# Two quarters of M made in one stay of TensorE, and keys asked for three steps ahead of their transposes

## The chip, the core and the metric

The kernel runs on one core of a Trainium2 chip. The metric is the time of one execution in microseconds, taken on the device, as the median of the runs shown. The profile is one further execution, recorded by the hardware profiler; its times are microseconds from the start of its span. The engines are called by the profile's names: PE (matmuls) and PEld (its weight loads), DVE, ACT and POOL (elementwise work), SP (here the issuer of the DMAs; its queue is SPq).

## What is computed

Eight batches of attention with 8 heads of 64, 576 tokens each, in two stages, and a feed-forward layer behind it. `p` holds 32 queries for each head.

```python
import numpy as np

def sm_attn(qq, kk, vv):
    s = scale * np.matmul(qq, kk.transpose(0, 1, 3, 2))
    s = s - np.max(s, axis=-1, keepdims=True)
    a = np.exp(s)
    a = a / (np.sum(a, axis=-1, keepdims=True) + 1e-09)
    return np.matmul(a, vv)

p_packed = sm_attn(p, k, v)                # 32 rows for each head
out = sm_attn(q, p_packed, p_packed)       # 576 rows for each head
x = out.transpose(0, 2, 1, 3).reshape(B * S, H * D)      # 4608 x 512
h = x @ w_in                               # 512 x 2048
relu6 = np.clip(h + 3.0, 0.0, 6.0)
y = (h * relu6 / 6.0) @ w_out              # 2048 x 512
```

All inputs and the output are float32.

## The kernel before

**Algebra.** Since `out` is a weighted sum of 32 packed rows for each head, `x @ w_in` is computed as attention weights times **M**, where M is the packed rows times `w_in` (256 x 2048 for each batch, as 8 heads of 32 rows). M is made in four **quarters** of 512 columns, n = 0 to 3. `u_m` (L528) makes a quarter: PE multiplies the packed rows (`pps`) with a quarter of `w_in` in `each_head` (L336, the matmul is L350), in its shape of 64x32 rows and columns, in 16 small matmuls, which the profile shows as 16 records. Such a visit of PE to this shape is called a **stay** here. Then two copies for each of two PSUM banks follow: ACT writes `m_hi` (L537), DVE the remainder `m_lo` (L539). The same `each_head` also makes scores of keys and queries with 288 columns in a stay.

**A batch.** The batches are worked one after the other; the work of batch b + 1's attention and M is laid in between the steps of batch b. A batch has two chunks of tokens, c = 0 and 1, and each chunk 16 steps, one for every 128 columns of d_ff; s = 16c + f counts the 32 steps. In even batches chunk 0 has 256 tokens (narrow) and chunk 1 has 320 (wide); in odd ones it is the other way round. A step begins with `fill` (L1401), which calls what is laid in there. Then PE makes the first product (`first_product` L922, matmul L929: attention weights as `a_hi`, `a_lo` times `m_hi`, `m_lo`, six matmuls) in one of two PSUM tiles, ACT and DVE make the gate h * relu6(h + 3) out of it (L940, L941), and the second product with `w_out` follows two or more steps later (L969). Twelve of the steps form six **pairs** (`moe_pairs` L1106), whose second products go through combined weights, as in a Strassen step: `wt` tiles T1, T2 and T4 of a pair. Of these `wt1` and `wt2` change hands: `FETCHES` (L29 to L33) and `fetch_t` (L1103, L1104) bring 768 KB from DRAM (`t_kept`) into `wt2` at step 5 and into `wt1` at step 7 of chunk 0, and back in chunk 1. Gates of a pair are t (first step) and tb (second step); ge, gf and ga are their parts that PE takes. Chunk 0 takes the pairs from the last to the first, so pairs 5 and 4 come first.

**M of the next batch.** A quarter of `w_in` is fetched anew for each batch from a copy in DRAM, 1 MB (`fetch_w_in` L1378, L1380, tile `w_again`, for which there is one place). `first_quarters` (L1382) fetches quarters 2, 1 and 0, each followed by its stay and its copies; `fill` takes one part of it at every step from 21 on (the stays come at steps 23, 28 and 31), and at step 31 all that is left of it, and then fetches quarter 3. Quarter 3's stay and its copies come as `late` at steps 1 to 3 of the next batch.

**Keys and queries.** `attention_inputs` (L558) loads the keys of the batch after, four times 4 DMAs of 72 KB (L294, tile `nat`, two places), and DVE transposes each into a tile `tr` (L555, four places): the loads of keys 0 and 1 stand at step 0, the four transposes at steps 1 to 4, the load of keys 2 and 3 behind the transposes of keys 0 and 1. Queries follow in the same tiles.

**What sets the order.** The program is written in steps, but the order of the instructions on each engine, SP's queue among them, is settled by a scheduler when the kernel is built, except where the matmuls of a stay or second products are placed by hand. Each engine then works its queue in order and waits at the head of it.

## Time and profile before

| what | before |
|---|---|
| runs, us | 712.67, 714.36, 715.0 |
| median, us | 714.36 |
| profiled execution, us | 714.05 |
| its span, us | 712.3 |
| PE busy, us and instructions | 690.8, 5906 |
| DVE busy | 533.8, 1164 |
| ACT busy | 429.5, 1015 |
| POOL busy | 349.7, 542 |

The span is the stretch between the first and the last instruction that the profiler saw; the execution's own time is a little longer. Busy time is the sum of an engine's durations without overlap. The page's row of slices (40 of 17.8 us) shows PE at 60% and 50% in the first two and at 90% or more in all behind them but the last, at 70%; its clock row stands at 9 tenths or more from the third on. In a row of a timeline the first two numbers are start and duration, then come engine, line, operation, output<-input tiles, form and count; a bracket at the end holds how long the engine had been idle ahead of it, and who ended that. A line "DMA to landing" gives the time from the issue of DMAs to the arrival of their data. A wait row reads: engine, tile and line, who was waited for, us in total, how often, the longest.

### The profile page before, as it was taken

How to read it: one execution, taken by the hardware profiler on the slowest of the kernel's cores; microseconds unless marked ns; L12 is line 12 of the kernel's file. 1: busy time of each engine (PE TensorE's matmuls, PEld its weight loads, DVE VectorE, ACT ScalarE, POOL GpSimd, SP SyncE). 2: the span in 40 equal slices, each digit the busy share in tenths (PEclk: the TensorE clock that was granted, in tenths of full speed). 3: DMA queues.
4: the chain of work that ended last, by engine and by line, in shares of the span. 5: the costliest groups of instructions: out<-in, count | busy, mean ns of one | idle time of the engine just before them, and what ended most of it. 6: DMA issues, size and time to landing. Idle time of an engine off the chain costs nothing.

```text
span 712.3 us, 16083 instructions
## 1 busy us (share of the span) xinstructions
PE 690.8 (97%) x5906; PEld 593.8 (83%) x5906; DVE 533.8 (75%) x1164; ACT 429.5 (60%) x1015; POOL 349.7 (49%) x542
## 2 busy tenths in 40 slices
PE   6599999999999999999999999999999999999997
PEld 4377877887878988899898988889898898889997
DVE  2887788688999769886598867887488776975453
ACT  5798876455565656566465655657366564756453
POOL 1565542545353454465353544556354444547553
PEclk9699999999999999999999999999999999999999
DMA  9989853955237756474454657375543845331030
GB/s 281 301 222 230 230 128 117 262 146 133 96 119 184 172 140 213 112 171 94 115 203 128 160 119 215 119 155 130 127 164 119 169 119 178 119 134 46 31 104 29
DMA packets 199102, 107.48 MB, mean 151 GB/s; under 512 B 173424, under 2 KB 185200, under 8 KB 195440
## 3 DMA queue, kind: packets, MB, share of 16 engines
...
q10 hardware_dynamic: 544, 0.20, 0.1%
...
## 4 chain that ended last, share of the span: by engine, by line
PE 75%; DVE 7%; DMA 3%; ACT 2%; issue 1%; SPq 1%; POOL 1%; DVEq 0%; ACTq 0%
PE acc L969 42%; PE ps_hh L929 23%; PE ps L350 6%; PE ps L969 2%; DVE tr L555 1%; PE ps L470 1%; PE ps_h L607 1%; DMA raw_out<-in_moe_w_out_dram 1%; DVE wt L1076 1%; DMA nat<-in_q_dram 1%; DMA w_again<-w_kept 1%; DMA nat<-in_k_dram 1%; SPq L294 1%; PE ps L440 0%; ACT wt L1075 0%
## 5 line engine op out<-in xcount | busy, mean ns | idle before, releaser
L929 PE MATMUL ps_hh<-a_hi,m_hi 128*128 128x320 f32 (+1 forms) x448 | 134.0, 299 | 0.6 <-DVE tb L941 0.4
L929 PE MATMUL ps_hh<-a_lo,m_hi 128*128 128x320 f32 (+1 forms) x448 | 133.3, 298 | 0.0
L929 PE MATMUL ps_hh<-a_hi,m_lo 128*128 128x320 f32 (+1 forms) x448 | 132.8, 296 | 0.0
L941 DVE SCALAR_TENSOR_TENSOR t<-t,ps_hh 128x320 f32<-128x320 f32 (+1 forms) x148 | 65.9, 446 | 56.4 <-ACT t L940 55.8
L947 POOL TENSOR_TENSOR gf<-tb,gf 128x256 fp32r<-128x256 f32 x76 | 64.2, 845 | 88.0 <-ACT gf L946 51.9
L969 PE MATMUL acc<-wo_hi,g 128*128 128x512 f32 x288 | 103.3, 401 | 0.0
L940 ACT ACTIVATE t<-ps_hh,three 128x320 f32<-128x320 f32 (+1 forms) x148 | 73.8, 500 | 32.4 <-PE ps_hh L929 27.3
L929 PEld LDWEIGHTS ps_hh<-a_hi,m_hi 128*128 128x128 f32 x448 | 84.6, 189 | 8.4 <-DVE t L941 1.9
L929 PEld LDWEIGHTS ps_hh<-a_lo,m_hi 128*128 128x128 f32 x448 | 84.7, 189 | 6.5 <-issue 3.5
L929 PEld LDWEIGHTS ps_hh<-a_hi,m_lo 128*128 128x128 f32 x448 | 84.5, 189 | 2.9 <-issue 2.5
L947 POOL TENSOR_TENSOR g<-t,g 128x256 fp32r<-128x256 f32 x72 | 54.8, 763 | 45.4 <-ACT g L946 24.4
L969 PE MATMUL acc<-wt,ga 128*128 128x256 f32 x456 | 74.7, 284 | 0.5 <-ACT ga L946 0.4
L969 PE MATMUL acc<-wo_hi,ge 128*128 128x256 f32 x304 | 71.8, 287 | 1.0 <-ACT ge L946 0.8
L947 POOL TENSOR_TENSOR ga<-t,ga 128x256 fp32r<-128x256 f32 x76 | 62.3, 820 | 13.5 <-ACT ga L946 12.3
L969 PEld LDWEIGHTS acc<-wt,ga 128*128 128x128 f32 x456 | 63.0, 190 | 3.7 <-ACT ga L946 1.7
L969 PEld LDWEIGHTS acc<-wo_hi,g 128*128 128x128 f32 x288 | 53.1, 188 | 13.0 <-POOL g L947 3.4
L969 PEld LDWEIGHTS acc<-wo_hi,ge 128*128 128x128 f32 x304 | 52.9, 190 | 9.6 <-DVE t L941 2.5
L969 PE MATMUL acc<-wo_lo,g 128*128 128x512 f32 x144 | 57.0, 396 | 0.0
L965 POOL COPY bnd<-t 128x64 f32<-128x64 f32 x76 | 22.3, 294 | 69.3 <-DVE t L941 66.5
L555 DVE STREAM_TRANSPOSE tr<-nat 128x576 f32<-128x576 f32 x56 | 42.3, 763 | 16.9 <-DMA nat<-in_q_dram 11.7
L940 ACT ACTIVATE tb<-ps_hh,three 128x256 f32<-128x256 f32 (+1 forms) x76 | 37.9, 498 | 19.4 <-PE ps_hh L929 18.4
L947 POOL TENSOR_TENSOR edge<-bnd,edge 128x256 fp32r<-128x256 f32 (+1 forms) x50 | 32.8, 662 | 32.2 <-ACT edge L946 32.2
...
## 6 DMA issues: line engine op xcount, KB each, us to landing
w_again<-w_kept SPq DMA_DIRECT2D x24, 1024.0 KB, 4.9
...
w_kept<-w_in_sb SPq DMA_DIRECT2D x4, 1024.0 KB, 8.9
```

Source lines behind the costliest of these rows:

```text
L294: nc.sync.dma_start(out=t[r:r + 32], in_=src[b, 2 * a + h, :, 32 * c:32 * c + 32].rearrange("(t i) j -> i t j", i=32),)
L350: nc.tensor.matmul(pair[x][NPK * a:NPK * a + NPK, :n], rows[half, a], c, start=True, stop=True)
L470: nc.tensor.matmul(pair[x][cols, :D], l, r, start=(c == 0), stop=(c == NST - 1))
L555: nc.vector.transpose(out=t, in_=state.pop(("nat", which, b, a)))
L607: nc.tensor.matmul(h[:, hf, :HS], mm[:, g, fs], aa[:, hf * HS:(hf + 1) * HS], start=(g == 0 and i == 0), stop=(g == NG - 1 and i == 2),)
L929: state["first"] = nc.tensor.matmul(h[:, :n], mm[:, g, fs], aa[:, t0:t0 + n], start=(g == 0 and i == 0), stop=(g == NG - 1 and i == 2),)
L940: state["relu"] = nc.scalar.activation(out=t[:, :n], in_=h, func=AF.Relu, bias=three)
L941: state["gate"] = nc.vector.scalar_tensor_tensor(out=t[:, :n], in0=t[:, :n], scalar=6.0, in1=h, op0=ALU.min, op1=ALU.mult)
L947: engine.tensor_sub(out=lo, in0=x, in1=hi.bitcast(F32))
L965: nc.gpsimd.tensor_copy(out=bnd[:, f, side * REM:side * REM + REM], in_=t[:, boff:boff + REM])
L969: nc.tensor.matmul(out, lhs[x], rhs[y], start=first and i == 0, stop=last and i == 2, skip_group_check=True)
L1076: nc.vector.tensor_sub(out=lo, in0=made, in1=hi.bitcast(F32))
```

## The change

Quarter 2 of the next batch's M is fetched at step 22, its stay moves to step 24, its copies to steps 27 and 28. Quarters 1 and 0 are fetched at step 24, right behind that stay. Quarter 1 goes into the tiles of the transposed keys and queries, which become one tile of four parts (`all_turned`), quarter 0 into the place of `w_again`. At step 31 both are multiplied in one stay, quarter 1 in two spare banks. One copy pair of quarter 1 follows at the same step, the other at step 0 of the next batch, those of quarter 0 at steps 2 and 3; quarter 3 is fetched at step 4, and has its stay at step 6 and its copies at 7 and 8. For b > 2 the keys' transposes start two steps later, at step 3 instead of 1, while the loads of keys 0 and 1 stay at step 0. Batch 1's M is made as before.

```diff
--- before.py
+++ after.py
@@ -24,6 +24,7 @@
 LATE = (3, 2, 1, 2, 1)
+SOON = (22, 24, 27, 28, 31, 31)
 PAIRS = 6
@@ -285,6 +286,18 @@
+    shared = []
+
+    def all_turned():
+        return ap.tile([P, 4, S], F32, name="tr", tag="tr", bufs=1)
+
+    def turned_room():
+
+        if not shared:
+            t = all_turned()
+            shared.extend(t[:, i] for i in range(4))
+        return shared.pop(0)
...
@@ -551,7 +564,7 @@
     def turn(which, b, a):
-        t = ap.tile([P, T, 32], F32, name="tr", tag="tr", bufs=4)
+        t = turned_room().rearrange("p (t n) -> p t n", n=32)
         nc.vector.transpose(out=t, in_=state.pop(("nat", which, b, a)))
@@ -561,6 +574,9 @@
         load("k", b, 0)
         load("k", b, 1)
         yield
+        if b > 2:
+            yield
+            yield
         transpose_p(b)
...
@@ -878,7 +894,7 @@
         def in_tr():
-            return ap.tile([P, 4 * P], F32, name="rows0", tag="tr", bufs=4)
+            return turned_room()[:, :4 * P]
@@ -1375,28 +1391,39 @@
-    def fetch_w_in(n):
-        t = w_in_sb[n] = wr.tile([P, FPC, NPAIR, P], F32, name="w_again", tag="w_in0")
+    def fetch_w_in(n, turned=False):
+        if turned:
+            t = all_turned().rearrange("p i n -> p (i n)")[:, :FPC * DM]
+            t = t.rearrange("p (f a e) -> p f a e", f=FPC, a=NPAIR)
+        else:
+            t = wr.tile([P, FPC, NPAIR, P], F32, name="w_again", tag="w_in0")
+        w_in_sb[n] = t
         nc.sync.dma_start(out=t.rearrange("p f a e -> p (f a e)"), in_=w_kept[n])
 
-    def first_quarters(b):
-
-        for n in range(NCH - 2, -1, -1):
-            fetch_w_in(n)
-            yield
-            yield
-            yield from coarse(u_m(b, n))
-
+    def quarters(b):
+
+        fetch_w_in(2)
+        yield
+        parts = coarse(u_m(b, 2))
+        next(parts)
+        fetch_w_in(1, True)
+        fetch_w_in(0)
+        yield
+        yield from parts
+        yield from coarse(u_m(b, 0, 1))
+        fetch_w_in(NCH - 1)
+        yield
+        yield
+        yield from coarse(u_m(b, NCH - 1))
+
+    soon = coarse(part for n in range(1, NCH) for part in u_m(1, n))
     for b in range(1, B):
         more = b + 1 < B
+        late, soon = soon, quarters(b + 1) if more else iter(())
...
         if b == 1:
-            late = coarse(part for n in range(1, NCH) for part in u_m(1, n))
             turned = [combine(i) for i in range(PAIRS)]
-        else:
-            late = coarse(u_m(b, NCH - 1))
-        soon = first_quarters(b + 1) if more else iter(())
...
-                    if s > 0:
+                    if s != 1:
                         next(late, None)
...
-                if s >= 21:
+                for _ in range(SOON.count(s)):
                     next(soon, None)
-                if s == 31 and more:
-                    rest(soon)
-                    fetch_w_in(NCH - 1)
```

Three places show what the order becomes. Rows name line, operation, output<-input with the tiles' numbers, and the shape; the diff moves later lines down by 13 to 16, so L350 of before is L363, L929 is L945, L941 is L957, L969 is L985 and L555 is L568.

**PE at the end of batch 2.** Before, around the stay of quarter 0 for batch 3; `g2` are the gates of batch 2's last single steps, `ps_hh` the first products of batch 3:

```order
L969 MATMUL acc_3598<-wo_lo_723,g2_3951 128x512
L969 MATMUL acc_3602<-wo_hi_722,g2_3951 128x512
L969 MATMUL acc_3602<-wo_lo_723,g2_3951 128x512
L350 MATMUL ps2_4007<-w_again_4005,pps_83 32x512 x8
L969 MATMUL acc_3598<-wo_hi_722,g2_3951 128x512
L969 MATMUL acc_3602<-wo_hi_722,g2_3951 128x512
L929 MATMUL ps_hh_4062<-a_hi_3728,m_hi_3773 128x320
L929 MATMUL ps_hh_4062<-a_lo_3729,m_hi_3773 128x320
```

After, at the same place:

```order
L985 MATMUL acc_3579<-wo_lo_719,g2_3956 128x512
L363 MATMUL ps_x_3968<-tr_3750,pps_83 32x512
L363 MATMUL ps_x_3967<-tr_3750,pps_83 32x512
L363 MATMUL ps_x_3968<-tr_3750,pps_83 32x512
L363 MATMUL ps_x_3967<-tr_3750,pps_83 32x512
L363 MATMUL ps_x_3968<-tr_3750,pps_83 32x512
L363 MATMUL ps_x_3967<-tr_3750,pps_83 32x512
L363 MATMUL ps_x_3968<-tr_3750,pps_83 32x512
L363 MATMUL ps_x_3967<-tr_3750,pps_83 32x512
L363 MATMUL ps2_3966<-w_again_3752,pps_83 32x512 x8
L985 MATMUL acc_3575<-wo_hi_718,g2_3956 128x512
L985 MATMUL acc_3579<-wo_hi_718,g2_3956 128x512
L945 MATMUL ps_hh_4050<-a_hi_3693,m_hi_3836 128x320
```

The stay of quarter 1, which stood 62 rows earlier, now goes ahead of quarter 0's with no full matmul between them.

**DVE at the start of batch 2.** Before, from behind the first gate `t_2870` of the batch to the end of that pair's gates; `p_tr` is the transpose of `p`, `wt2` and `wx` belong to the making of the combined weights, `osb` to the output of batch 1:

```order
L1196 TENSOR_TENSOR t_2870<-t_2870 128x128
L322 STREAM_TRANSPOSE p_tr_2895<-p_nat_2848 128x128
L555 STREAM_TRANSPOSE tr_2897<-nat_2853 128x576
L1095 TENSOR_TENSOR wx_2743<-wx_2743,wo_lo_723 128x256
L941 SCALAR_TENSOR_TENSOR tb_2911<-tb_2911,ps_hh_2904 128x256
L1167 SCALAR_TENSOR_TENSOR osb_2645<-acc_2421,osb_2645 128x512
L947 TENSOR_TENSOR ge_2874<-t_2870,ge_2874 128x256
L1167 SCALAR_TENSOR_TENSOR osb_2646<-acc_2425,osb_2646 128x512
L1204 TENSOR_TENSOR t_2870<-t_2870,tb_2911 128x2x128
L1076 TENSOR_TENSOR wt2_1789<-wx_2743,wt2_1789 128x256
L941 SCALAR_TENSOR_TENSOR t_2952<-t_2952,ps_hh_2945 128x256
L1209 TENSOR_TENSOR tb_2911<-tb_2911,t_2870 128x128
```

After, from the same gate `t` on:

```order
L957 SCALAR_TENSOR_TENSOR t_2845<-t_2845,ps_hh_2838 128x256
L1111 TENSOR_TENSOR wx_2718<-wx_2718,wo_lo_719 128x256
L1212 TENSOR_TENSOR t_2845<-t_2845 128x128
L1092 TENSOR_TENSOR wt2_1777<-wx_2718,wt2_1777 128x256
L963 TENSOR_TENSOR ge_2849<-t_2845,ge_2849 128x256
L957 SCALAR_TENSOR_TENSOR tb_2865<-tb_2865,ps_hh_2858 128x256
L1183 SCALAR_TENSOR_TENSOR osb_2628<-acc_2406,osb_2628 128x512
L1220 TENSOR_TENSOR t_2845<-t_2845,tb_2865 128x2x128
L1183 SCALAR_TENSOR_TENSOR osb_2629<-acc_2410,osb_2629 128x512
L1225 TENSOR_TENSOR tb_2865<-tb_2865,t_2845 128x128
L552 TENSOR_TENSOR m_lo_2889<-ps2_2776,m_hi_2888 128x512
L957 SCALAR_TENSOR_TENSOR t_2899<-t_2899,ps_hh_2892 128x256
```

The transposes of `p` and of keys 0, which stood between the first gate and its `ge`, come behind these gates and those of the next pair (three and four rows further on; the second keys ten rows further on).

**DVE at the start of batch 4, after,** where keys 2 and 3 are transposed (`nat_5406` and `nat_5459`):

```order
L957 SCALAR_TENSOR_TENSOR tb_5492<-tb_5492,ps_hh_5485 128x256
L1220 TENSOR_TENSOR t_5471<-t_5471,tb_5492 128x2x128
L963 TENSOR_TENSOR ge_5475<-t_5471,ge_5475 128x256
L1225 TENSOR_TENSOR tb_5492<-tb_5492,t_5471 128x128
L568 STREAM_TRANSPOSE tr_5404<-nat_5406 128x576
L957 SCALAR_TENSOR_TENSOR t_5558<-t_5558,ps_hh_5551 128x256
L1212 TENSOR_TENSOR t_5558<-t_5558 128x128
L552 TENSOR_TENSOR m_lo_5566<-ps2_5526,m_hi_5565 128x512
L568 STREAM_TRANSPOSE tr_5404<-nat_5459 128x576
L963 TENSOR_TENSOR ge_5562<-t_5558,ge_5562 128x256
L957 SCALAR_TENSOR_TENSOR tb_5577<-tb_5577,ps_hh_5570 128x256
L1220 TENSOR_TENSOR t_5558<-t_5558,tb_5577 128x2x128
```

Before, these two stood two steps earlier; now they are ahead of the gates of the fourth pair that PE takes.

**SP at the start of batch 3.** Before, from the fetch of quarter 3 (`w_again_4025`) on; `nat` are keys and queries, `v_nat` values, `osb` the output:

```order
L1380 DMA w_again_4025<-w_kept_1573 128x2048
L294 DMA nat_4099<-in_k_dram 32x18x32 x4
L1170 DMA out_0_dram<-osb_3976 128x512
L1170 DMA out_0_dram<-osb_3977 128x512
L294 DMA nat_4141<-in_k_dram 32x18x32 x4
L294 DMA nat_4165<-in_q_dram 32x18x32 x4
L419 DMA v_nat_4223<-in_v_dram 128x4x64 x2
L294 DMA nat_4218<-in_q_dram 32x18x32 x4
L419 DMA v_nat_4223<-in_v_dram 128x4x64 x2
L409 DMA v_nat_4223<-in_v_dram 64x4x64 x2
L1104 DMA wt2_1789<-t_kept_1574 128x1536
```

After:

```order
L1401 DMA w_again_4157<-w_kept_1564 128x2048
L1186 DMA out_0_dram<-osb_3939 128x512
L1186 DMA out_0_dram<-osb_3940 128x512
L1120 DMA wt2_1777<-t_kept_1565 128x1536
L307 DMA nat_4106<-in_k_dram 32x18x32 x4
L307 DMA nat_4160<-in_k_dram 32x18x32 x4
L432 DMA v_nat_4247<-in_v_dram 128x4x64 x2
L307 DMA nat_4182<-in_q_dram 32x18x32 x4
L307 DMA nat_4242<-in_q_dram 32x18x32 x4
L432 DMA v_nat_4247<-in_v_dram 128x4x64 x2
L422 DMA v_nat_4247<-in_v_dram 64x4x64 x2
L1120 DMA wt1_1776<-t_kept_1565 128x1536
```

Keys 2 and 3 (`nat_4106`, `nat_4160`) now stand behind the fetch of `wt2`, which stood behind keys, queries and values before; the starts of batches 2, 4, 5 and 6 have the same order.

## The prediction

> **What bounds the kernel now.** I read the page's engine shares first, then the chain that ended last, then the windows of PE by batch, and only then single rows.
>
> ```profile
> span 712.3 us, 16083 instructions
> PE 690.8 (97%) x5906; PEld 593.8 (83%) x5906; DVE 533.8 (75%) x1164; ACT 429.5 (60%) x1015; POOL 349.7 (49%) x542
> PE 75%; DVE 7%; DMA 3%; ACT 2%; issue 1%; SPq 1%; POOL 1%; DVEq 0%; ACTq 0%
> 551.00:635.00 84.00, 83.72 (x752) 1.00 0.52 143
> L350 PE MATMUL ps<-w_again,pps 64*32 64x512 f32 x384 | 26.1, 601 | 0.0
> ```
>
> PE is busy for 690.8 of 712.3 us and carries 75% of the chain. The window row (PE's busy time as sum and mean with its instructions, its clock, the DMA share, GB/s) is one whole batch of 84 us: PE has gaps of 0.3 us in it, at full clock. So a microsecond counts only if PE issues less, or if PE stops waiting. Batch time hides small waits, because a modelled duration overlaps the next start; I therefore count from start to start. The last row is the work that the change regroups: the stays of PE in its 64x32 shape that make M, 24 of 16 records each.
>
> **Part 1, the merged stay.** What a stay costs is read between the last full matmul ahead of it and the second one behind it.
>
> ```profile
> 385.70 0.28 PE L929 MATMUL ps_hh<-a_lo,m_hi 128*128 128x256 f32 x1
> 385.82 0.28 PE L929 MATMUL ps_hh<-a_hi,m_lo 128*128 128x256 f32 x1
> 386.02 1.09 PE L350 MATMUL ps<-w_again,pps 64*32 64x512 f32 x16
> ...
> 387.27 0.28 PE L969 MATMUL acc<-wo_lo,ge 128*128 128x256 f32 x1
> ...
> 399.99 0.28 PE L929 MATMUL ps_hh<-a_hi,m_lo 128*128 128x256 f32 x1
> 400.20 0.72 PE L350 MATMUL ps<-tr,p_tr 64*32 64x288 f32 x16
> ...
> 401.07 0.28 PE L969 MATMUL acc<-wo_lo,gf 128*128 128x256 f32 x1
> ```
>
> ```profile
> 56.01 0.39 PE L969 MATMUL acc<-wo_hi,gl 128*128 128x512 f32 x1
> 56.33 0.71 PE L350 MATMUL ps_w<-tr,p_tr 64*32 64x288 f32 x16
> ...
> 57.80 0.40 PE L969 MATMUL acc<-wo_lo,gh 128*128 128x512 f32 x1
> 58.03 0.39 PE L969 MATMUL acc<-wo_hi,gl 128*128 128x512 f32 x1
> ```
>
> A 256-column matmul follows the next at 0.12 us (385.70 to 385.82), a 512-column one at 0.23 (57.80 to 58.03). One M stay is thus (387.27 − 0.12) − (385.82 + 0.12) = 1.21 us. One stay of 288 columns is (401.07 − 0.12) − (399.99 + 0.12) = 0.84. The trace of before has no two M rounds in one stay, but it has two rounds of 288 columns in one (the second, left out, is 16 records too): (57.80 − 0.23) − (56.01 + 0.23) = 1.33 us, against 2 x 0.84 = 1.68. The second round saves 0.35 us, the price of entering and leaving the shape once. That does not depend on the columns, so two M rounds in one should take 2 x 1.21 − 0.35 = 2.07. The change merges quarters 0 and 1 for b = 2 to 7: 6 x 0.35 = **−2.1 us**, bounds 0 (all comes back, rival 3) and −2.1.
>
> The work the merged stay issues is otherwise the same: the same 32 records, the same four copies. The fetches stay the same three megabytes; from quarter 2's stay at step 24 to the merged one at step 31 there are seven steps of 84/32 = 2.6 us, and a fetch lands in 4.9:
>
> ```profile
> w_again<-w_kept SPq DMA_DIRECT2D x24, 1024.0 KB, 4.9
> ```
>
> Two behind one another are some 10 us against 18: hidden. Quarter 3's fetch waits for the merged stay and has from step 31 to step 6, seven steps again. I cost the fetches at nothing.
>
> **Part 2, waits that the new times remove.** At the start of b = 2, PE waits for gates that stand on DVE behind three key transposes (the first and the last of them below) and copies of quarter 0.
>
> ```profile
> 216.87 0.28 PE L929 MATMUL ps_hh<-a_hi,m_lo 128*128 128x256 f32 x1
> 217.75 0.39 PE L969 MATMUL acc<-wo_hi,ge 128*128 128x256 f32 x1 [0.60 <-ACT ge L946]
> ...
> 223.03 0.32 PE L969 MATMUL acc<-wo_hi,ga 128*128 128x256 f32 x1
> 223.56 0.39 PE L969 MATMUL acc<-wo_hi,ge 128*128 128x256 f32 x1 [0.20 <-ACT ge L946]
> ...
> 224.00 0.28 PE L969 MATMUL acc<-wo_lo,ge 128*128 128x256 f32 x1
> 224.71 0.39 PE L929 MATMUL ps_hh<-a_hi,m_hi 128*128 128x256 f32 x1 [0.43 <-DVE tb L941]
> ```
>
> ```profile
> 217.40 0.74 DVE L555 STREAM_TRANSPOSE tr<-nat 128x576 f32<-128x576 f32 x1
> ...
> 222.66 0.40 DVE L1196 TENSOR_TENSOR t<-t 128x128 f32<-128x128 f32 x1
> 222.99 0.76 DVE L555 STREAM_TRANSPOSE tr<-nat 128x576 f32<-128x576 f32 x1
> 223.69 0.64 DVE L539 TENSOR_TENSOR m_lo<-ps,m_hi 128x512 fp32r<-128x512 f32 x1
> ```
>
> Start to start, less 0.12 each, PE lost 0.76 at 216.87, 0.41 at 223.03 and 0.59 at 224.00: 1.8 us. By the new order on DVE the first key transpose comes behind the first two gates of that start, and the third and fourth leave the stretch altogether. The combine's own rows stay in it. I take 1.3 of the 1.8 as gone (bounds 0 and 1.8): **−1.3**.
>
> At the start of b = 6 the third keys were late:
>
> ```profile
> 556.98 0.78 DVE L555 STREAM_TRANSPOSE tr<-nat 128x576 f32<-128x576 f32 x1 [1.61 <-DMA nat<-in_k_dram]
> 558.01 0.28 PE L969 MATMUL acc<-wo_hi,ge 128*128 128x256 f32 x1
> ...
> 561.08 0.74 PE L969 MATMUL acc<-wt,ga 128*128 128x256 f32 x4 [0.22 <-ACT ga L946]
> ```
>
> From 558.01 to 561.08 stand 18 matmuls of 256 columns, some 2.1 us at their pace; 0.9 us was lost behind a DVE wait of 1.61. That transpose now comes elsewhere: **−0.9** (its new place is priced in part 3).
>
> In b = 1, chunk 1, a gate stood behind a slow subtraction:
>
> ```profile
> 194.04 1.29 DVE L524 TENSOR_TENSOR a_lo<-at,a_hi 128x576 fp32r<-128x576 f32 x1
> 195.91 0.39 PE L969 MATMUL acc<-wo_hi,ga 128*128 128x256 f32 x1 [0.65 <-ACT ga L946]
> ```
>
> The new order has the small subtraction that this gate needs (L1209 TENSOR_TENSOR) ahead of it: **−0.6**, bounds 0 and the row's 0.65. Parts 1 and 2 are −4.9.
>
> **Part 3, the wait that the change adds.** Keys 2 and 3 are now loaded for a transpose at steps 5 and 6, and in five transitions (b = 2 to 6) SP has the wt2 fetch directly ahead of them. That fetch waits until PE has used wt2 for pair 5; call that time T. Of loads behind a wt fetch and of loads alone the trace says:
>
> ```profile
> L1104 SPq DMA_DIRECT2D wt<-t_kept x1: 547/547/547, 232.5 to 232.5; - x1
> L294 SPq DMA_DIRECT2D nat<-in_q_dram x4: 376/488/1092, 233.1 to 234.6; - x4
> DMA to landing us min/median/max: 5.2/5.2/5.3
> L294 SPq DMA_DIRECT2D nat<-in_k_dram x8: 333/494/519, 384.1 to 389.3; - x8
> DMA to landing us min/median/max: 2.1/2.4/2.7
> ```
>
> Four loads right behind the fetch took 5.2 us each, eight with nothing ahead 2.4. The last of the four landed at 234.6 + 5.3 = 239.9, 7.4 us after the fetch was issued. So keys 2 land at up to T + 7.4; behind them DVE has, at the durations quoted, the transpose 0.77, a gate 0.41, L1212 0.40, m_lo 0.64, the transpose of keys 3 0.76 and then ge, 0.4: T + 10.8. When does PE want that ge?
>
> ```profile
> 389.63 0.52 PE L969 MATMUL acc<-wt,ga 128*128 128x256 f32 x3
> 398.92 0.28 PE L969 MATMUL acc<-wo_hi,ge 128*128 128x256 f32 x1
> ```
>
> In b = 4 pair 5's last wt product starts by 389.63 + 2 x 0.12 and the ge of the third pair behind it at 398.92: 9.0 us later. Quarter 3's stay, which now comes in between, adds 1.21: T + 10.2. PE would be kept 0.6 us at a start with narrow chunks; a wide one gives PE some more time for its first products. Bounds for each start: 0, and 2.0 (the whole DVE wait of some 2.6, were DVE at that place at T + 4.8, less the 1.61 − 0.9 = 0.7 that b = 6 absorbed). Against the upper end stands this row, where DVE waited for queries behind the same fetch in windows in which PE lost nothing:
>
> ```profile
> DVE tr L555 <- DMA nat<-in_q_dram: 11.7, 11, 1.9
> ```
>
> I take 0.6 for each of five: **+3.0**.
>
> The Trainium skill, page "DMA: Bandwidth & Descriptors", section "Queues, rings and completion order", says that SP owns one row of rings, that descriptors of one ring are taken in order, and that a semaphore increment lands only after every earlier write of that DMA engine. By it the keys' semaphores cannot come before the fetch's data, so no start escapes the late landing; the rows above agree with it (5.2 against 2.4). By it the waits of DVE are certain, and only PE's lead decides between the forecast's +3.0, nothing and rival 2's +10.
>
> **Sum.** Against the profiled run, 714.05 us (span 712.3 and 1.75 around it): 714.05 − 2.1 − 1.3 − 0.9 − 0.6 + 3.0 = **712.2 us**. The median of the runs shown, 714.36, is 0.3 above the profiled one; 0.3%, or 2.1 us, is about what a measurement of this kernel can tell from no change, and the forecast lies on that edge.
>
> **The rivals.**
>
> Rival 1, the waits for keys are hidden. If PE's lead covers the late landing, as it did for the queries, the 3.0 go: 709.2 us. For it: the row of 11 waits; wide starts have more lead. Against it: keys come nearer to the start of the batch, where b = 6 paid.
>
> Rival 2, slower: the wt2 fetch ahead of the keys holds DVE in all five starts and PE pays in full. At 2.0 each it is +10: 714.05 − 4.9 + 10 = 719.2 us. It turns the sum above no change by 2.1 us when a start costs (4.9 + 2.1 + 0.3)/5 = 1.5 us or more, which is a landing some 0.9 later than the T + 7.4 reckoned, or a DVE queue that is as much longer. For it: the 5.2 us row and b = 6.
>
> Rival 3, the merged stay gives nothing. Both quarters' four banks wait for their copies at once, at a batch's start, where DVE has also two output rows of 0.68 to do (their place in the trace is that of 216 to 224 above). One m_lo is 0.64 on DVE, so two more of them ahead of a gate are 1.3 us; if 0.35 of it reaches PE each time, the 2.1 us are spent: 714.3 us. The Trainium skill, page "TensorEngine Tiling (Array Packing)", section "Performance Considerations", warns that tiling speeds TensorE but not the emptying of PSUM; by it this is where a merged stay would lose, and no row of before shows four banks at once.
>
> Rival 4, the starts only trade their waits: the 1.3 and 0.6 of part 2 turn up a few rows later. 712.2 + 1.9 = 714.1 us.
>
> **How the numbers follow.** Forecast 0.38, half of it on each side of 712.2; rival 1 0.22; rival 2 0.13; rival 3 0.10; rival 4 0.17. Faster by over 0.3%: 0.19 + 0.22 = 0.41. Slower by over 0.3%: 0.13 and a little of rivals 3 and 4, 0.14. The rest, 0.45, is within 0.3%. The forecast's own range is 710.7 to 713.7 (a start at 0.3 to 0.9). For 8 in 10 the range takes in rival 1 down to 708.6 and stops between rivals 3 and 2, at 716.4; left out are rival 2's 0.13 and the far end of rival 1.
>
> **What would show it.** In the changed trace a timeline of PE around the merged stay should show 32 records and about 2.07 us between full matmuls; 2.4 would make part 1 wrong. The waits view should name DVE's transpose behind in_k_dram about ten times instead of five, and DMA to landing of the key loads should rise from 2.4 to about 5 at steps 3 to 5 of b = 2 to 6; PE's starts there should stretch by 0.3 to 0.9. If keys land at 2.4, or DVE waits and PE does not stretch, rival 1 is right; if PE stretches by over 1.5 in each, rival 2. PE's gaps at 217 to 225 should have shrunk to 0.5 in all, and the 0.65 at 195.9 should be gone; if they only moved, rival 4. What would make the whole wrong is a new wait that I have not priced: the tile that quarter 1 is fetched into is one room for all four transposes, so its fetch waits for the last query products, and the keys for the merged stay.

## The result: slower, and outside the range

| | before | after |
|---|---|---|
| runs | 6 | 6 |
| median, us (lowest to highest) | 713.64 (712.49 to 715.0) | 718.42 (717.99 to 720.02) |
| profiled execution, us | 714.05 | 717.99 |
| its span, us | 712.3 | 716.2 |

The ratio after to before is 1.0077, 95% interval 1.0062 to 1.0092. Forecast were 712.2 us and a range from 708.6 to 716.4.

The page of the kernel after: busy time by engine, the shares of the chain that ended last, and three rows of DMA issues with the median time to landing.

```profile
span 716.2 us, 16090 instructions
PE 690.8 (96%) x5906; PEld 594.2 (83%) x5906; DVE 529.4 (74%) x1164; ACT 427.7 (60%) x1015; POOL 354.4 (49%) x542
...
PE 53%; DVE 11%; DMA 2%; issue 1%; ACT 1%; POOL 1%; SPq 1%; DVEq 0%; ACTq 0%
...
w_again<-w_kept SPq DMA_DIRECT2D x18, 1024.0 KB, 5.1
...
nat<-in_k_dram SPq DMA_DIRECT2D x112, 72.0 KB, 4.6
```

PE issues the same 690.8 us of work as before and the span is 3.9 longer, so PE waits more. Its share of the chain falls from 75% to 53%: others release it. The loads of keys take 4.6 us to land, where before they took 3.2. In the list of DVE's waits they now hold the second place, with ten waits where there were five. The first row is of before, the second of after:

```profile
DVE tr L555 <- DMA nat<-in_k_dram: 4.8, 5, 1.6
DVE tr L568 <- DMA nat<-in_k_dram: 16.8, 10, 2.6
```

Below, a **loss** of PE is the time from one matmul's start to the next beyond the usual pitch of its form, summed over a place. Such a sum is good to some 0.1 at a place, since the first matmul behind a wait or a stay also starts its follower about 0.1 late. Losses in us behind 125 us of the span:

| place | before | after |
|---|---|---|
| batch 1 (158 to 200) | 4.1 | 2.2 |
| start of b = 2 | 2.4 | 2.3 |
| keys at the starts of b = 2 to 6 | 1.1 (b = 6 alone) | 4.9 (0.74, 1.52, 0.67, 1.00, 0.96) |
| ends of b = 2, 4, 6 | 0 | 4.7 (1.58, 1.57, 1.58) |
| 412 to 418 in b = 4 | 0.7 | 0.2 |

With six merged stays (−2.1) and 0.4 gained ahead of the first product of the attention weights (`ps_hh`, at 118.8 before and 118.5 after) this makes +3.5 of the span's +3.9; 0.4 is spread too thin to be placed. The 0.4 ahead of that product is scatter as far as can be told: over all the profiled executions of this document it starts anywhere from 117.3 to 120.3.

**The merged stay,** PE's timeline after, around the end of b = 2 (start, duration):

```profile
290.80 0.39 PE L985 MATMUL acc<-wo_lo,g 128*128 128x512 f32 x1
291.12 1.09 PE L363 MATMUL ps_x<-tr,pps 64*32 64x512 f32 x16
292.00 1.06 PE L363 MATMUL ps<-w_again,pps 64*32 64x512 f32 x16
293.00 0.73 PE L985 MATMUL acc<-wo_hi,g 128*128 128x512 f32 x2
293.57 0.30 PE L945 MATMUL ps_hh<-a_hi,m_hi 128*128 128x320 f32 x1
```

(293.57 − 2 x 0.23) − (290.80 + 0.23) = 2.08 us for 32 records; 2.07 was forecast.

**A start with late keys,** b = 3 after: SP's queue, then DVE, then PE.

```profile
300.11 0.33 SPq L1120 DMA_DIRECT2D wt<-t_kept  x1
300.52 5.65 SPq L307 DMA_DIRECT2D nat<-in_k_dram  x8
...
307.14 0.78 DVE L568 STREAM_TRANSPOSE tr<-nat 128x576 f32<-128x576 f32 x1 [2.08 <-DMA nat<-in_k_dram]
310.11 0.78 DVE L568 STREAM_TRANSPOSE tr<-nat 128x576 f32<-128x576 f32 x1 [1.82 <-DMA nat<-in_k_dram]
...
311.55 0.39 PE L985 MATMUL acc<-wo_hi,ge 128*128 128x256 f32 x1 [0.74 <-ACT ge L962]
```

With T the issue of the wt fetch, keys 2 come at T + 7.0, keys 3 at T + 10.0, and DVE waits twice, with the gates of PE's next product queued behind. The second row shows why keys 3 come so much later: SP takes 5.65 us to issue the eight loads, so that the last is issued at T + 5.6, and it lands 4.4 later.

**An end of an even batch,** b = 4 after: DVE around the last pair's gates, then PE.

```profile
448.53 0.68 DVE L552 TENSOR_TENSOR m_lo<-ps,m_hi 128x512 fp32r<-128x512 f32 x1
449.13 0.47 DVE L957 SCALAR_TENSOR_TENSOR tb<-tb,ps_hh 128x320 f32<-128x320 f32 x1
449.53 0.75 DVE L528 TENSOR_TENSOR z<-z,den 128x576 f32<-128x576 f32 x1
450.20 0.79 DVE L537 TENSOR_TENSOR a_lo<-at,a_hi 128x576 fp32r<-128x576 f32 x1
450.91 0.95 DVE L963 TENSOR_TENSOR ge<-t,ge 128x256 fp32r<-128x256 f32 x1
...
450.95 0.40 PE L985 MATMUL acc<-wt,gf 128*128 128x256 f32 x2
451.63 0.38 PE L985 MATMUL acc<-wo_hi,gf 128*128 128x256 f32 x1 [0.28 <-POOL gf L963]
...
451.96 0.45 PE L985 MATMUL acc<-wo_hi,ge 128*128 128x256 f32 x2
452.68 0.74 PE L985 MATMUL acc<-wt,ga 128*128 128x256 f32 x4 [0.27 <-ACT ga L962]
```

Two products at 0.12 each behind 450.95 make the next due at 451.19; it came at 451.63, 0.44 late, and the one at 452.68 was 0.48 late. The brackets show 0.28 and 0.27 of it. DVE has no gap there; between the gate `tb` and `ge` it does 1.4 us of the next batch's softmax (`z`, `a_lo`). Why these ends lose is the question of most of the experiments.

### The profile page after: what moved, and what is told of

It is laid out like the page before. It is cut to its first block, busy times and chain, and to the rows that moved or that the text cites. A ratio compares the mean times of both kernels' runs of the same rounds, so it can differ in the third digit from the quotient of the medians.

```text
span 716.2 us, 16090 instructions
## 1 busy us (share of the span) xinstructions
PE 690.8 (96%) x5906; PEld 594.2 (83%) x5906; DVE 529.4 (74%) x1164; ACT 427.7 (60%) x1015; POOL 354.4 (49%) x542
## 4 chain that ended last, share of the span: by engine, by line
PE 53%; DVE 11%; DMA 2%; issue 1%; ACT 1%; POOL 1%; SPq 1%; DVEq 0%; ACTq 0%
PE acc L985 30%; PE ps_hh L945 16%; PE ps L363 3%; DMA nat<-in_k_dram 2%; PE ps L985 2%; DVE ge L963 1%; DVE tb L957 1%; DVE t L1220 1%; DVE tb L1225 1%; PE ps L483 1%; DVE m_lo L552 1%; PE ps_x L363 1%; DVE z L517 1%; PE ps L453 1%; DMA out_dram<-osb 1%
## 5 line engine op out<-in xcount | busy, mean ns | idle before, releaser
L945 PE MATMUL ps_hh<-a_hi,m_hi 128*128 128x320 f32 (+1 forms) x448 | 135.1, 302 | 1.0 <-DVE t L957 0.9
L945 PE MATMUL ps_hh<-a_hi,m_lo 128*128 128x320 f32 (+1 forms) x448 | 132.7, 296 | 0.0
L945 PE MATMUL ps_hh<-a_lo,m_hi 128*128 128x320 f32 (+1 forms) x448 | 132.6, 296 | 0.0
L963 POOL TENSOR_TENSOR gf<-tb,gf 128x256 fp32r<-128x256 f32 x76 | 67.2, 885 | 82.8 <-ACT gf L962 68.4
L985 PE MATMUL acc<-wo_hi,g 128*128 128x512 f32 x288 | 102.1, 399 | 0.0
L957 DVE SCALAR_TENSOR_TENSOR t<-t,ps_hh 128x320 f32<-128x320 f32 (+1 forms) x148 | 65.5, 445 | 48.6 <-ACT t L956 47.6
L945 PEld LDWEIGHTS ps_hh<-a_hi,m_hi 128*128 128x128 f32 x448 | 84.6, 189 | 8.7 <-DVE t L957 3.3
L945 PEld LDWEIGHTS ps_hh<-a_lo,m_hi 128*128 128x128 f32 x448 | 84.7, 189 | 2.3
L945 PEld LDWEIGHTS ps_hh<-a_hi,m_lo 128*128 128x128 f32 x448 | 84.6, 189 | 0.4
L985 PE MATMUL acc<-wt,ga 128*128 128x256 f32 x456 | 75.7, 284 | 0.8 <-ACT ga L962 0.8
L985 PE MATMUL acc<-wo_hi,ge 128*128 128x256 f32 x304 | 71.6, 287 | 2.4 <-DVE ge L963 1.3
L963 POOL TENSOR_TENSOR ga<-t,ga 128x256 fp32r<-128x256 f32 x76 | 60.3, 793 | 20.5 <-ACT ga L962 20.4
L985 PEld LDWEIGHTS acc<-wt,ga 128*128 128x128 f32 x456 | 63.7, 190 | 4.0 <-ACT ga L962 1.4
L568 DVE STREAM_TRANSPOSE tr<-nat 128x576 f32<-128x576 f32 x56 | 42.4, 764 | 28.9 <-DMA nat<-in_k_dram 16.8
L985 PEld LDWEIGHTS acc<-wo_hi,g 128*128 128x128 f32 x288 | 52.6, 188 | 13.4 <-issue 4.2
L985 PEld LDWEIGHTS acc<-wo_hi,ge 128*128 128x128 f32 x304 | 53.1, 190 | 9.5 <-DVE t L1212 3.4
L985 PE MATMUL acc<-wo_lo,g 128*128 128x512 f32 x144 | 57.0, 396 | 0.0
L962 ACT CAST ge<-t 128x256 fp32r<-128x256 f32 x76 | 30.9, 406 | 36.1 <-DVE t L1212 35.3
```

What stands on the lines that cost most here:

```text
L568: nc.vector.transpose(out=t, in_=state.pop(("nat", which, b, a)))
L945: state["first"] = nc.tensor.matmul(h[:, :n], mm[:, g, fs], aa[:, t0:t0 + n], start=(g == 0 and i == 0), stop=(g == NG - 1 and i == 2),)
L957: state["gate"] = nc.vector.scalar_tensor_tensor(out=t[:, :n], in0=t[:, :n], scalar=6.0, in1=h, op0=ALU.min, op1=ALU.mult)
L962: nc.scalar.copy(out=hi, in_=x)
L963: engine.tensor_sub(out=lo, in0=x, in1=hi.bitcast(F32))
L985: nc.tensor.matmul(out, lhs[x], rhs[y], start=first and i == 0, stop=last and i == 2, skip_group_check=True)
```

## The experiments

| run | change to what | median, us (runs) | ratio to the kernel before, 95% | keys at starts | ends of b = 2, 4, 6 |
|---|---|---|---|---|---|
| after | | 718.42 (6) | 1.0077, 1.0062 to 1.0092 | 4.9 | 1.58, 1.57, 1.58 |
| e1 | after, keys back | 720.34 (4) | 1.0103, 1.0073 to 1.0133 | 7.4 with quarter 3 | 0, 1.59, 1.58 |
| e2 | after, wt fetch behind keys | 714.53 (10) | 1.0018, 0.9999 to 1.0037 | 0.5, and 3.0 for wt | 1.59, 0, 0 |
| e3 | after, copies earlier | 718.10 (6) | 1.0060, 1.0040 to 1.0081 | 6.3 | 1.08, 1.14, 1.14 |
| e4 | e2 and e3 | 715.78 (10) | 1.0033, 1.0014 to 1.0053 | | 1.08 each |
| e5 | after, softmax a step later | 716.79 (4) | 1.0040, 1.0025 to 1.0055 | | 1.67, 1.67, 1.76 |
| e6 | e2, queries behind wt1 | 711.54 (5) | 0.9966, 0.9952 to 0.9979 | 0.3 | 1.59, 0, 0 |
| e7 | e5 and e6 | 711.60 (10) | 0.9979, 0.9966 to 0.9992 | | 1.73 at b = 2 |
| e8 | after, merge undone | 718.99 (4) | 1.0075, 1.0045 to 1.0105 | | 1.20, 1.19, 1.18 |
| e9 | after, softmax held 2 steps | 718.31 (4) | 1.0078, 1.0055 to 1.0100 | | 1.80 each |
| e10 | e6, the same at b = 2 | 711.43 (12) | 0.9979, 0.9966 to 0.9991 | | 1.76 at b = 2 |
| e11 | e6, merge undone | 712.36 (12) | 0.9979, 0.9967 to 0.9992 | | |
| e12 | e6, softmax a step earlier | 717.78 (6) | 1.0052, 1.0035 to 1.0069 | | 1.73, 1.72, 1.73 |
| e13 | after, ACT's order | 721.66 (4) | 1.0126, 1.0093 to 1.0158 | 8.7 | 1.60, 1.54, 1.60 |
| e14 | e6, the same | 711.46 (10) | 0.9977, 0.9963 to 0.9991 | | 1.59 at b = 2 |
| e15 | after, scores first on DVE | 719.89 (4) | 1.0092, 1.0073 to 1.0112 | 6.9 | 1.19, 1.20, 1.19 |
| e16 | e6, the same | 711.31 (10) | 0.9974, 0.9960 to 0.9987 | | 1.19 at b = 2 |
| e17 | after, less work on DVE | 717.22 (5) | 1.0045, 1.0029 to 1.0061 | | 1.58, 1.58, 1.62 |
| e18 | after, last gates first | 713.67 (10) | 0.9999, 0.9980 to 1.0017 | 5.4 | 0, 0, 0 |

The losses are read from each one's profiled execution, one for each kernel; an empty cell was not summed. The theories are named by letters in the expectations.

**The starts.** e1 drops the two steps by which the keys come later:

```diff
-        if b > 2:
-            yield
-            yield
```

> The changed kernel without the two steps of delay for the keys' transposes (they stand at steps 1 to 4 again); merged stay and the new times of the quarters are kept. In the changed kernel's trace PE loses 4.9 us at five starts (230, 311, 400, 480, 569 us) where DVE waits for keys 2 and 3. Theory A (the delay puts the key loads behind the wt2 fetch): these five losses go, the waits of DVE for keys fall from 16.8 to under 8 us, and the median comes to about 714 (718.4 - 4.9, and up to 1 back for the starts that the early transposes burden). Theory B (the starts lose time because of the merged stay's copies and quarter 3's stay at step 6, whenever keys come): the starts keep most of the 4.9 us, median 717 to 718.5. The loss of 4.7 us near the end of batches 2, 4 and 6 (281, 451, 621 us) stays in both.

It became slower. Loads of keys 3 now stand behind quarter 3's fetch (b = 4: 6.2 us to landing at most), DVE waits up to 4.2 for them, and quarter 3's stay waits for its own fetch:

```profile
391.60 1.09 PE L363 MATMUL ps<-w_again,pps 64*32 64x512 f32 x16 [1.13 <-DMA w_again<-w_kept]
```

So the later keys do not cause the loss by themselves; they make room for a quarter 3 that is fetched at step 4. e2 leaves them and takes away what stands ahead of them:

```diff
+                if src is k:
+                    state["keys"] = load
...
-                            fetch_t(i)
+                            with tc.issue_after(state["keys"].ins):
+                                fetch_t(i)
```

> The changed kernel with one edge more: the wt2 fetch of chunk 0 is issued behind the last load of keys 3, instead of ahead of keys 2. The transposes stay two steps later. Theory A (DVE waits because the keys' data queues behind the fetch): keys land 2.4 to 3 us after issue instead of 4.6 (median of all), DVE's waits for keys fall from 16.8 to under 5 us, PE's losses at the five starts fall from 4.9 to under 1, median about 713.8. Theory B (the two transposes and two copies are too much work for DVE ahead of the fourth pair's gates, wait or no wait): the waits go, PE still loses 3 us or more at the five starts, median 716.5 to 718. A wait for wt2 in its turn (PE for wt of pair 1) would show as a new bracket in PE's timeline ten steps into these batches.

For the loads of keys in b = 4 the trace after has the first of these rows, e2's the second:

```profile
DMA to landing us min/median/max: 3.6/5.2/5.2
```

```profile
DMA to landing us min/median/max: 2.2/2.4/3.0
```

The median falls to 2.4, and the starts lose 0.5 in place of 4.9. The fetch of wt1 now comes late in turn, behind queries and values, and PE loses 3.0 us by it in b = 2, 4 and 6. One of these, b = 4:

```profile
410.99 0.39 PE L987 MATMUL acc<-wt,gf 128*128 128x256 f32 x1 [1.19 <-DMA wt<-t_kept]
```

e6 also has wt1 fetched at step 6 instead of 7, and for b > 2 the queries 0 and 1 and the low values behind it:

```diff
-FETCHES = (((5, 1), (7, 0)), ((5, 4), (7, 5)))
+FETCHES = (((5, 1), (6, 0)), ((5, 4), (7, 5)))
...
+            with tc.issue_after(state["wt"].ins):
+                load("q", b, 0)
+                load("q", b, 1)
+                load_v_low(b)
```

> e2 (wt2 fetch behind keys 3) with the wt1 fetch at step 6 instead of 7, and queries 0 and 1 and the low values loaded behind it. In e2 the wt1 fetch was issued late behind queries and values, and PE waited for wt (0.34, 1.35 and 0.97 us in batches 2, 4 and 6). Theory A, the SP queue's order at a batch's start decides: these 2.7 us go, nothing new comes, median 711.5 to 712.5. Rival: the queries, now landing behind 768 KB more, delay DVE or the scores of queries, and the time is given back: median 714 to 715.

It beats both kernels. DVE still waits ten times for keys, and PE loses nothing by it:

```profile
DVE tr L570 <- DMA nat<-in_k_dram: 8.5, 10, 1.9
```

**The merge.** e8 gives quarter 1 its own stay again, at step 30, in the kernel after; e11 does so in e6.

```diff
-SOON = (22, 24, 27, 28, 31, 31)
+SOON = (22, 24, 27, 28, 30, 31, 31)
...
-        yield from coarse(u_m(b, 0, 1))
+        one, zero = coarse(u_m(b, 1, spare=True)), coarse(u_m(b, 0))
+        next(one)
+        yield
+        next(zero)
...
```

> The changed kernel with the merged stay undone: quarter 1's round has a stay of its own at step 30, in the same two spare banks, quarter 0's at step 31; fetches, copies, keys and the SP queue's order as in the changed kernel. If the merge saves what the trace reads (two stays of 1.21 us against one of 2.08, six times): 2.1 us more than the changed kernel, 720.5. If the merged stay costs at the copies what it saves on PE (rival 3 of the prediction): no change or faster, 717.5 to 718.5. Losses at starts and ends should stay as in the changed kernel.

> e6 with the merge undone as in e8 (stays of quarters 1 and 0 at steps 30 and 31). In the changed kernel the same edit moved the median by 0.6 us, less than its runs could tell from nothing, because other losses moved with it. Here, where starts and ends lose little, the merge should be seen alone: 711.5 + 2.1 = 713.6 if it saves what the stays read; 711.5 to 712 if its four banks of copies cost what it saves.

e8 is 0.6 slower than after, e11 0.8 slower than e6, both inside their intervals, where 2.1 was to be lost. In e8 the ends lose 0.4 less each and the start of b = 2 loses 1.62 instead of 2.26, together 1.8 that come back. The traces say more than these medians. One row for each of after, e8, e6 and e11, in this order; after the durations it has the start of the first and of the last product of this kind:

```profile
L945 PE MATMUL ps_hh<-a_hi,m_hi x448: 277/303/417, 118.5 to 707.4; 128*128 128x320 f32 x75, 128*128 128x256 f32 x75
L945 PE MATMUL ps_hh<-a_hi,m_hi x448: 277/303/417, 117.3 to 708.0; 128*128 128x320 f32 x75, 128*128 128x256 f32 x75
L954 PE MATMUL ps_hh<-a_hi,m_hi x448: 277/303/416, 119.1 to 701.2; 128*128 128x320 f32 x75, 128*128 128x256 f32 x75
L954 PE MATMUL ps_hh<-a_hi,m_hi x448: 277/303/417, 118.1 to 702.3; 128*128 128x320 f32 x75, 128*128 128x256 f32 x75
```

From the first to the last, e8 takes 1.8 us longer than after (590.7 against 588.9) and e11 2.1 longer than e6 (584.2 against 582.1). Of e8's 1.8, some 0.8 lie in batch 1, ahead of the first stay that the edit touches, so e11 and e6 are the cleaner pair. In e11 about 0.4 arises at each of the ends of b = 3 to 6, nothing at b = 2, whose end loses 0.4 less, and 0.6 at the start of b = 4. So the stay takes what was forecast. The kernel gains it, in this pair, at ends where PE waits for nothing behind the stay; at an end that loses, undoing the merge takes as much off the loss.

**The ends: the copies.** e3 puts quarter 2's copies at steps 25 and 26; e4 does so in e2, and its median is 1.25 above e2's.

```diff
-SOON = (22, 24, 27, 28, 31, 31)
+SOON = (22, 24, 25, 26, 31, 31)
```

> The changed kernel with quarter 2's copies at steps 25 and 26 instead of 27 and 28. In the changed kernel PE loses 1.58 us in each of batches 2, 4 and 6 at step 27 to 28 (281, 451 and 621 us), 4.7 in all; the forecast had no term for it. Theory C (the copies' two m_lo, 0.68 us each on DVE, stand there among the normalisation of the next batch's attention, and push the last pair's gates): the three losses shrink to under 0.5 each, median 714 to 715. Theory D (the normalisation itself stands earlier against PE, because PE has fewer stays ahead of it there; the copies' place does not matter): the losses stay, median 717.5 to 718.5.

> The edits of e2 and e3 together: wt2 fetch behind the keys, quarter 2's copies at 25 and 26. By A and C the gains add, 4.9 - 1 and 4.7 - 1.5: about 710 to 711, faster than the kernel before by 0.4 to 0.5%. By A and D about 713.8, by B and C about 714 to 715, by B and D 717 to 718.

In e3 some 30% of the loss at the ends goes, and the starts lose 1.4 more. e4's ends lose as e3's do, but its profiled execution was the slowest of its ten (720.67), and in it the three waits of PE for wt1 are 5.5 us together where e2's are 2.2. The longest of them, and PE's row of windows behind it (length, busy, clock, DMA share, GB/s):

```profile
412.96 0.80 PE L987 MATMUL acc<-wt,gf 128*128 128x256 f32 x2 [3.72 <-DMA wt<-t_kept]
...
413.00:415.00 2.00, 2.00 (x9) 0.50 0.81 132
```

So e4 does not show whether the two gains add.

**The ends: when the softmax comes.** e5 begins the making of the next weights at step 20 instead of 19, e12 (from e6) at 18. e9 holds it at step 26 and does two parts at 28; e7 and e10 try e5 and e9 in e6, without a difference.

```diff
+                    if chain is ahead and b % 2 == 0:
+                        count = {26: 0, 28: 2}.get(s, count)
```

> The changed kernel with one number changed: the normalisation of the next batch's second attention starts at step 20 instead of 19 (for batches from 2 on). By the new order DVE has the last pair's ge and t in batches 2, 4 and 6 ahead of the product z and the subtraction a_lo (0.75 and 0.79 us) again, as in the kernel before; quarter 2's copies stay at 27 and 28. Theory D (the order of that normalisation against the last pair's gates costs the 4.7 us; e3 moved the copies alone and 1.1 of 1.58 stayed in each): the losses at about 281, 451 and 621 us fall under 0.5 each, median 714 to 715. Theory C2 (DVE is simply full there, whatever the order): the losses stay at 1 us or more each, median 717 to 718.5. The losses for the keys, 4.9 us, stay in both.

> e5 and e6 in one kernel. If both theories hold: no key wait, no wt wait, and no loss at the ends of batches 2, 4 and 6 (e2 and e6 have it in batch 2 alone, 1.6 us): median 710 to 711, 0.3 to 0.4% below the kernel before, whose merged stay, worth 2.1 us, it lacks. If the starts or the ends keep a loss that I have not named: 713 or more.

> The changed kernel with one step of the next batch's normalisation held back in batches 2, 4 and 6 (none at step 26, two at 28). SP's queue is the same row for row; DVE's order differs from the changed kernel's only at the ends of these three batches, where ge and t of the last pair now stand ahead of the product z; one a_lo still stands ahead of the gate tb. e5 moved the whole chain by a step, put z and a_lo ahead of another gate, and the losses moved with them (0.40 and 0.67 us where 0.43, 0.43 and 0.30 had been), while in e2 and e6 the same work in another order lost nothing in batches 4 and 6. Theory D: the losses of 1.58 us fall to 0.5 or less in each, median 714.5 to 715.5. Theory C2 (DVE is too full there in any order): 1 us or more stays in each, median 717 or more.

> e6 with the edit of e9 in batch 2 alone, the one even batch whose end still lost 1.59 us in e6. By D: 711.5 - 1.2 = 710.3, the best of all these; by C2 711.5 as e6.

> e6 with the next batch's query scores and normalisation started at step 18 instead of 19. The reorderings of e3, e5 and e9 only moved the losses at the ends of batches 2, 4 and 6; what the kernels without a loss there (before, and e6 in batches 4 and 6) have in common is that the first half's subtraction a_lo runs by 445 us in batch 4 (444.8 and 443.2), some 8 us ahead of the second half's; in the changed kernel, e3 and e9 it runs at 450, 4 us ahead of it, so that both halves' last operations fall among the last pair's gates. Theory E (the two halves' ends bunch there; DVE needs the chain earlier, whatever the rest of the order): with one step (some 2.6 us) more time the end of batch 2 loses under 0.5 us instead of 1.59, batches 4 and 6 stay without loss: 710 to 710.5. If batches 4 and 6 now lose as well (both a_lo stand ahead of the last pair's ge in all three by the new order): 711.5 to 713, and E is wrong: the place against those gates decides, not the time.

Each left a loss of 1.7 to 1.8 at the ends, e12 even at those of b = 4 and 6, where e6 had none; e12 also loses 3.3 us in the second half of b = 3 (357 to 374), where e6 loses nothing.

**The ends: ACT's order.** In the kernel after (b = 4) ACT stood idle for 1.01 us in front of a cast, with the last pair's first relu behind it:

```profile
446.60 0.30 ACT L962 CAST ga<-tb 128x128 fp32r<-128x128 f32 x1 [1.01 <-DVE tb L1225]
446.81 0.52 ACT L956 ACTIVATE t<-ps_hh,three 128x320 f32<-128x320 f32 x1
```

e13 has this relu ahead of the cast, e14 does so in e6:

```diff
+                    while held:
+                        with tc.issue_after(state["relu"].ins):
+                            held.pop()()
...
+                if c == 1 and even and f // 2 == pairs[-2]:
+                    held.append(lambda lhs=lhs, x=x, s4=s4: parted(lhs, ("S4",), x[:, 4 * P:], s4.unsqueeze(1)))
...
```

> The changed kernel, and in even batches, chunk 1, the last part of pair 4's gates (the small subtraction's result, `ga<-tb`, cast on ACT and its remainder on POOL) is issued behind the first relu of pair 5, where the changed kernel has it ahead. Everything computed is the same. At the ends of b = 2, 4 and 6 PE loses 1.58, 1.57 and 1.58 us in the changed kernel; there ACT stands idle 1.01 us at 445.6 to 446.6 in front of that cast, while the relu queued behind it has had its first product since about 445.1. Theory F (ACT's head of queue: the cast waits for DVE's L1225, and the relu of the last pair waits behind the cast, so the last pair's whole chain of gates is some 1.5 us late): relu of the last pair starts at about 445.3 instead of 446.8, each end loses 0.5 or less, and the time falls by some 3.5 to 4.7 us, to 714 to 715. Rival G (DVE is full there in any case, and what it does not do late it must do early): the relu comes earlier, but DVE reaches the gates no sooner; the ends lose 1.2 or more, here or within 10 us, and the time stays at 717.5 or more.

> e6 with the same edit of ACT's order at the ends of even batches. In e6 only the end of b = 2 loses (1.6 us, ACT idle 1.00 in front of `ga<-tb` at 276.9 to 277.9); b = 4 and b = 6 lose nothing. Theory F: the end of b = 2 loses 0.5 or less, some 1.2 us in all, 710.3. Rival G: no change at b = 2, and the new order may cost up to 1.5 at the ends of b = 4 and 6, which were free: 711.5 to 714.

The order is as wanted, the ends lose as much, and the new order costs more at the starts. Theory F fell.

**The ends: where the scores come on DVE.** In all traces so far the loss went with the second scores' place behind a gate. e15 puts them ahead, e16 in e6:

```diff
+                with tc.issue_after(state["z"].ins) if even and c == 1 and pos == 7 else ExitStack():
+                    gate_into(tb, h, n)
...
```

> The changed kernel, and in even batches DVE's gate of step 23 (`tb`, L957) is issued behind the transposes that take the second half of the query scores out of PSUM (`z<-ps`), where the changed kernel has them behind that gate and two more rows. Everything computed is the same. In the traces so far the second `z<-ps` starts 0.87 us behind its stay at the ends that lose nothing (the best version's b = 4 and 6, e1's b = 2), 1.31 in the kernel before, and 1.74 at every end that loses 1.1 to 1.8 (the changed kernel's b = 2, 4, 6 and those of e3, e5, e9, e12, e13). Theory S (DVE is full from there on, and what decides is whether its softmax starts ahead of that gate or behind it): the ends of b = 2, 4 and 6 lose 0.5 or less each, 3.5 to 4.7 us fewer in all; the time falls to 714 to 715, unless the new order takes something elsewhere. Rival T (the late scores only go along with the loss; DVE has too much to do there in any order): the ends lose 1.1 or more each, the time stays at 717.5 or more.

> The best version (e6) with the same edit; there b = 4 and 6 have that order already, so that only b = 2 changes much. Theory S: its end loses 0.5 or less in place of 1.59, and the time is some 1.1 below e6, 710.4. Rival T: 1.1 or more, 711.5.

The ends lose 1.19 instead of 1.58: a quarter of the loss goes, and e16 loses 1.2 in return in b = 3 (368 to 374). What had gone along with the loss in every trace is at most a quarter of its cause.

**The ends: amount or order.** e17 takes 1.5 us of DVE's work away in each of the batches 2, 4 and 6:

```diff
-        mx = sm.tile([P, T], F32, name="mx2")
+        if x == 0 or b < 3 or b % 2 == 0:
+            mx = sm.tile([P, T], F32, name="mx2")
...
```

> The changed kernel without the subtraction of the maximum in the second softmax of one half of the heads, for the weights of batches 3, 5 and 7 only (they are made during batches 2, 4 and 6): the rows `mx<-z` (0.75) and `z<-z,mx` (0.79) of one half are left out, 1.5 us of DVE in each of these batches, ahead of the ends that lose 1.58. SP's order is the same, and the other engines' orders differ only around these three ends. Theory H (DVE has too much to do between the second scores, at 435 in b = 4, and the end at 453; which row stands where matters little): each end loses 0.4 or less, some 3.5 to 4.7 us in all, 714 to 715. Rival O (the loss comes from the order, not from the amount): the ends lose 1.1 or more each, as after every other edit there, 717.5 or more.

The ends lose what they lost, in another place: a gate stands behind three rows of other work. DVE at b = 4 of e17, then PE:

```profile
449.05 0.75 DVE L538 TENSOR_TENSOR a_lo<-at,a_hi 128x576 fp32r<-128x576 f32 x1
449.72 0.32 DVE L1213 TENSOR_TENSOR t<-t 128x128 f32<-128x128 f32 x1
449.97 0.68 DVE L553 TENSOR_TENSOR m_lo<-ps,m_hi 128x512 fp32r<-128x512 f32 x1
450.57 0.77 DVE L532 STREAM_TRANSPOSE at<-z 128x576 f32<-128x576 f32 x1
451.26 0.45 DVE L958 SCALAR_TENSOR_TENSOR tb<-tb,ps_hh 128x320 f32<-128x320 f32 x1
...
451.76 0.42 PE L946 MATMUL ps_hh<-a_hi,m_hi 128*128 128x320 f32 x1 [0.48 <-DVE tb L958]
```

e18 takes no work away and moves such rows behind the last pair's gates, in batches 2, 4 and 6:

```diff
-                for _ in range(SOON.count(s)):
+                for _ in range((SOON if b % 2 else (22, 24, 28, 29, 31, 31)).count(s)):
...
+                    if chain is ahead and b in (2, 4, 6):
+                        n = {25: 0, 26: 0, 27: 0, 28: 3, 29: 2}.get(s, n)
```

> The changed kernel, and in batches 2, 4 and 6 nothing but one transpose and one `a_lo` is left on DVE ahead of the gates of the last pair, and nothing between them: the second softmax half waits from step 25 to step 28 (then three of its parts at once and two at step 29), quarter 2's copies come at steps 28 and 29 instead of 27 and 28. Everything computed is the same, no DVE work is taken away. Theory O (order: with some 2 us of rows of the softmax and of M in front of and between the last pair's gates, PE gets them too late; all edits so far left such rows there, e17 too, where `a_lo`, `m_lo` and `at` stood 2.0 us in front of a gate): the ends of b = 2, 4, 6 lose 0.5 or less each, 3.5 to 4.7 us fewer in all at these ends; the time 714 to 715 if the weights, which come later, hold up nothing in the next batch. Rival H (amount: DVE is full, and the work put off comes due behind the gates): 1.1 or more at the ends or within 15 us behind them, 717.5 or more.

DVE at the end of b = 4 in e18, PE behind the gates, and PE's row of windows:

```profile
446.45 0.48 DVE L957 SCALAR_TENSOR_TENSOR t<-t,ps_hh 128x320 f32<-128x320 f32 x1
446.96 0.29 DVE L1212 TENSOR_TENSOR t<-t 128x128 f32<-128x128 f32 x1
447.17 0.48 DVE L957 SCALAR_TENSOR_TENSOR tb<-tb,ps_hh 128x320 f32<-128x320 f32 x1
447.69 0.42 DVE L1220 TENSOR_TENSOR t<-t,tb 128x256 f32<-128x256 f32 x1
448.03 0.46 DVE L963 TENSOR_TENSOR ge<-t,ge 128x256 fp32r<-128x256 f32 x1
448.41 0.83 DVE L1225 TENSOR_TENSOR tb<-tb,t 128x128 f32<-128x128 f32 x1
449.16 0.68 DVE L552 TENSOR_TENSOR m_lo<-ps,m_hi 128x512 fp32r<-128x512 f32 x1
...
450.40 0.28 PE L985 MATMUL acc<-wt,gf 128*128 128x256 f32 x1
450.52 0.28 PE L985 MATMUL acc<-wo_hi,ge 128*128 128x256 f32 x1
450.63 0.88 PE L985 MATMUL acc<-wt,ga 128*128 128x256 f32 x6
451.35 0.28 PE L985 MATMUL acc<-wo_hi,ga 128*128 128x256 f32 x1
...
450.00:455.00 5.00, 5.00 (x34) 1.00 0.02 5
```

The six rows of the last pair stand together, PE goes on at its pitch of 0.12, and none of the three ends loses anything. The median is 4.75 us below after's. That this is the 4.7 of the ends is partly chance: in the profiled executions, from the first `ps_hh` product to the last, e18 takes 3.2 us less than after (117.7 to 703.4, so 585.7 against 588.9), because its starts and the rows behind them, of b = 2 and 3 above all, lose some 1.3 more. At the ends order is the cause, since the work is the same and the loss is gone; e18 and e6 in one kernel was not tried.

## Why the prediction was wrong

Against the profiled execution the forecast is 5.8 us short (717.99 − 712.2). The differences below, with −0.2 for b = 6, where 1.1 went instead of the 0.9 taken, sum to 5.3; 0.5 stays unplaced.

- **The ends, +4.7: a term that was missing.** The step that failed is "the same 32 records, the same four copies", with which part 1 took the work around the stays as unchanged; for quarter 2's copies at their new steps the sum has no term. The amount is unchanged; but quarter 2's copies and the next weights now meet the last pair of an even batch on DVE, and the scheduler put rows of both between its gates. Bringing the copies forward took 30% of it (e3); e18 shows that with another order of the same rows all of it goes. The prediction named an unpriced wait as what would make it wrong, and looked for it at the fetch of quarter 1, where there is none.
- **The starts, +1.9: part 3 was mis-sized.** Keys 2 at T + 7.4 was right (7.0). The step that failed is that keys 3 would be there when DVE had come so far: they landed at T + 10.0, and DVE waited a second time, 1.82 us in b = 3. The sum had the time that DVE needs for the rows in between and none for SP to issue four more loads. A start cost 0.67 to 1.52, 4.9 in all, for the 3.0 taken. The Trainium skill, page "DMA: Bandwidth & Descriptors", section "Queues, rings and completion order", was weighed there: a semaphore increment lands only behind every earlier write of that DMA engine. The runs agree (keys of b = 4 behind the fetch 5.2 us to landing, ahead of it 2.4). The rule says why no key lands ahead of the fetch, and not why keys 3 land 3.0 behind keys 2.
- **Rival 2** came nearest in time (719.2) with a mechanism that is half of its size: a start costs 1.0, not 2.0. That the time comes out near is chance: the ends, which it does not have, made up the rest. Its waits of DVE are there, and so is the way to take them off (e2, e6).
- **The merged stay, −2.1: right in place.** 2.08 for 2.07. What it is worth to the kernel is less sure: undone, the medians rise by 0.6 and 0.8 (e8, e11), within their scatter, and the traces by 1.8 and 2.1 behind the first product. Where an end loses anyway, some 0.4 of its loss goes when the two stays are apart, so that the merge gains nothing there. Rival 3 asked for such a give-back at the four banks' copies; the runs do not show which wait takes it.
- **The start of b = 2, +1.1.** Of the 1.3 taken as gone, 0.2 went. The waits at 216 to 224 are gone and others stand at 211 to 218, behind gates and the combine's rows; that is what rival 4 said. No run tests it. Batch 1 gave 1.3 more than the 0.6 taken, the waits at 412 to 418 another 0.5, the start-up 0.4; none of these was in the sum, and the last is within its scatter.
- **Fetches at nothing** was right for the quarters as the change has them. e1 shows how near it is: with the keys two steps earlier quarter 3's stay waits 1.13.
